# One attention and FFN kernel, two written-out orders of its work

## The chip, the cores and the metric

The kernel runs on one core of one Trainium2 chip. The core has five engines with queues of their own: TensorE (PE in the profile; its weight loads are PEld), VectorE (DVE), ScalarE (ACT), GpSimd (POOL) and SyncE (SP), which here only issues transfers. The metric is the device time of one execution in microseconds, the median over several executions.

## The reference

```
phi(x) = outer(S1 x, S2 x)            # 8 x 8 = 64 features of each 32-vector
kv  = sum_s phi(k_s) v_s              # per batch and head: 64 x 32
z   = sum_s phi(k_s)                  # 64
att = phi(q) kv / (phi(q) z + 1e-6)   # 4 batches, 4 heads, 1088 positions, 32 wide
x   = att as 4352 tokens x 128
out = (relu(x Wg) * (x Wv)) Wo        # Wg, Wv: 128 x 1536, Wo: 1536 x 128
```

Everything comes in and goes out as 32-bit floats. The FFN part runs on 16-bit operands.

## The kernel before

The work of a batch goes through stages. K: the keys are transposed on VectorE (`kt1`), multiplied with the sketches on TensorE (`ksk`), transposed back (`kt2`), multiplied to features (`kphi`, on VectorE or GpSimd), and multiplied with the values (`kv`); `kve` moves the result out of PSUM. `z`, `zc`, `w`, `wc` make the denominator's weights. Q: the same for queries (`qt1`, `qsk`, `qt2`), then `bw`, `red`, `rd`, `an` for the denominator, `qphi` for the features, a transpose (`qtr`, on TensorE or as a DMA), and `num`, whose result ScalarE writes as the FFN's input `x`. The first 512 tokens go through a shorter class of their own, `First`; its steps have an `f` ahead of their name (`f sk`, `f t2`, `f csk`, `f bw`, `f rx`, `f phi`, `f tr`, `f pt`, `f num`, `f xd`).

The FFN is cut into 102 units, numbered from 0; a unit is 512 columns of hidden work. Unit u has a gate product `g u` and a value product `v u` on TensorE, each into one PSUM bank, `relu u` on ScalarE, `h u` on VectorE (gate times value, straight from PSUM), and four output products `o u`. In 19 units ScalarE copies the value out (`vcp u`) and GpSimd multiplies (`hp u`). Units 0 to 23 hold 256 tokens and two column blocks, 24 to 95 hold 512 tokens and one. The three weights come in thirds: block 0 of each by SP in 32 bits, cast by ScalarE (`cw g0`, `cw v0`, `cw o0`, line 316); blocks 1 and 2 by GpSimd's queue (line 310). In a group of six units the first two need block 0, the next two block 1, the last two block 2.

Some lines of the profile: 367 is `st`, 370 `ws`, 375 `wq`, 491 `kt1`, 501 `ksk`, 507 `kt2`, 543 `kphi`, 654 `f sk`, 660 `f t2`, 680 `f bw`, 695 `f phi`, 780 `qsk`, 793 `qt2`, 848 `num`, 916 `g` and `v`, 921 `relu`, 925 `vcp`, 931 `h`, 936 `hp`, 944 `o`, 951 `oe`, 1015 the dummy products.

No planner runs when the kernel is built. Each step is added to a list of 857 with what it needs. A table `START` gives each step a place; all steps are issued in the order of these places, so the table fixes the order of every engine's queue at once. `BANKS` gives each of 268 uses of PSUM its bank or banks. `WARM` says before which steps TensorE gets dummy products: 128 x 128 zeros times zeros, whose result nobody reads:

```
def run(self, warm):
    order = sorted(self.ops, key=lambda o: (START[o.seq] if START else 0, o.seq))
    for o in order:
        if o.seq in WARM:
            warm(WARM[o.seq])
        o.fn()
```

An engine does its steps strictly in this order: one that must wait holds up all behind it. The step `gate` on GpSimd writes one element of a tile that the load of batch 1's keys overwrites, so SP's loads of batch 1 wait for it, and those of the later batches stand behind.

Of the kernel before, what the change touches and what calls it, by code (L numbers as in the profile page):

```python
# [29 lines left out]
Q0E = 'ACT'  # L30
RXE = ['ACT', 'DVE']
START = [
# [47 lines left out]
]  # L80
BANKS = [
# [19 lines left out]
]  # L101
WARM = {34: 29, 63: 2, 143: 14, 147: 1, 152: 9}


class Lease:
# [15 lines left out]
class Plan:  # L121
# [10 lines left out]
    def run(self, warm):  # L132
        assert not START or len(START) == len(self.ops)
# [919 lines left out]
```

## Time and profile before

| | |
|---|---|
| median of 3 executions | 101.69 us (101.67 to 102.08) |
| profiled execution, span from first to last instruction | 100.1 us |
| time around the span, median less span | 1.6 us (the page gives no other time of its own) |
| busy: PE, DVE, ACT, POOL | 94.2, 82.7, 84.1, 65.8 us |
| chain that ended last | PE 81%, ACT 6%, POOL 4%, DMA 3% |
| first FFN product | 14.58 us after the span's start |
| last product on PE begins its last run | 95.18 us; the last output copy on ACT at 96.62 us |

A busy PE is one with some product in flight. Products overlap, so a PE that is busy throughout can still do more in a stretch if its products follow closer. Times in the rows are counted from the span's start. What stands in brackets behind a row is idle time of that engine just before it, and what ended it.

### The profile page before, as it was taken

Reading aid. Unit: us, or ns where it says so; the run is one execution under the profiler, and the core shown is the slowest. Engines: PE = TensorE matmul, PEld = TensorE weight load, DVE = VectorE, ACT = ScalarE, POOL = GpSimd, SP = SyncE. Lnnn points to the kernel's source line nnn. Section 1 sums busy time; section 2 is a strip of 40 time slices with the busy share of each in tenths; the row PEclk is TensorE's granted clock in tenths of the full one; section 3 lists DMA queues with packets and bytes.
Section 4 is the critical chain, followed back from the end, with each engine's and each line's share of the span. In section 5 each row is a group of like instructions: output and inputs, shape, how many; then the busy total and the mean of one; then the engine's idle time right before and its main releaser. Section 6 shows DMA issues by size and latency. Waiting matters only on the chain.

```text
span 100.1 us, 3180 instructions
## 1 busy us (share of the span) xinstructions
PE 94.2 (94%) x1223; PEld 68.3 (68%) x1223; DVE 82.7 (83%) x175; ACT 84.1 (84%) x169; POOL 65.8 (66%) x89
## 2 busy tenths in 40 slices
PE   6999989989999999999999999999999999999950
PEld 6978969848779965557673656765676665688940
DVE  4778779999989998999998689799746879897940
ACT  3445889999799798998999999899999999998730
POOL 6029947898988999999897699935944404001700
PEclk9999999999999999999999999999999999999999
DMA  2988889999930525208664200071217305003331
GB/s 43 370 229 267 146 122 358 339 269 276 342 125 0 111 66 134 45 12 235 165 182 99 60 0 7 1 169 27 52 29 120 78 0 129 2 7 84 99 105 52
DMA packets 14799, 12.40 MB, mean 124 GB/s; under 512 B 8256, under 2 KB 12352, under 8 KB 14784
## 3 DMA queue, kind: packets, MB, share of 16 engines
q1 hardware_dynamic: 13392, 10.70, 38.5%
q0 software_dynamic: 864, 0.79, 5.8%
q10 hardware_dynamic: 528, 0.72, 2.2%
q8 instruction: 9, 0.15, 0.7%
q14 instruction: 6, 0.05, 0.2%
HBM read 9.05 MB, written 2.23 MB: 113 GB/s over the span
## 4 chain that ended last, share of the span: by engine, by line
PE 81%; ACT 6%; POOL 4%; DMA 3%; issue 1%; DVE 1%
PE ps L916 42%; PE ps L944 23%; PE ps L1015 5%; ACT g_sb L921 4%; DMA wg<-in_moe_w_gate_dram 3%; PE ps L848 3%; PE ps L501 2%; PE ps L780 2%; POOL kp L543 2%; PE ps L567 2%; ACT v_sb L925 1%; POOL fqp L695 1%; ACT qpt L840 1%; PE ps L515 1%; POOL wv L310 1%
## 5 line engine op out<-in xcount | busy, mean ns | idle before, releaser
L921 ACT ACTIVATE g_sb<-ps 128x512 f16<-128x512 f32 x102 | 56.3, 613 | 3.9 <-PE ps L916 3.2
L931 DVE TENSOR_TENSOR ht<-g_sb,ps 128x512 f16<-128x512 f16 (+1 forms) x84 | 53.5, 673 | 7.2 <-PE ps L916 5.6
L916 PE MATMUL ps<-xT,wv 128*128 128x512 f16 (+1 forms) x132 | 35.6, 332 | 0.5 <-ACT g_sb L921 0.5
L916 PE MATMUL ps<-xT,wg 128*128 128x512 f16 (+1 forms) x132 | 34.3, 332 | 0.3 <-DMA wg<-in_moe_w_gate_dram 0.3
L944 PEld LDWEIGHTS <-ht 128*128 128x128 f16 x408 | 28.0, 98 | 9.2 <-issue 0.8
L944 PE MATMUL ps<-wo,ht 128*128 128x128 f16 x408 | 33.8, 219 | 0.0
L936 POOL TENSOR_TENSOR ht<-g_sb,v_sb 128x512 f16<-128x512 f16 x19 | 21.7, 1158 | 16.4 <-ACT g_sb L921 14.9
L916 PEld LDWEIGHTS <-wg 128*128 128x128 f16 x132 | 13.6, 115 | 5.9 <-issue 2.2
L543 POOL TENSOR_TENSOR kp<-kab 128x512 f16<-128x512 f32 (+2 forms) x14 | 15.7, 1136 | 2.0 <-DVE kab L507 2.0
L916 PEld LDWEIGHTS <-wv 128*128 128x128 f16 x132 | 13.9, 114 | 3.6 <-issue 1.3
L821 POOL TENSOR_TENSOR qqp<-qan,qabc 128x1024 f16<-128x1024 f32 (+1 forms) x9 | 14.9, 1658 | 0.4
L925 ACT CAST v_sb<-ps 128x512 f16<-128x512 f32 x19 | 11.3, 601 | 0.6 <-PE ps L916 0.5
L1015 PE MATMUL ps<-zero 128*128 128x128 f16 x55 | 5.9, 285 | 1.0 <-DVE zero L292 1.0
L793 DVE STREAM_TRANSPOSE qabc<-ps 128x128 f32<-128x128 f32 (+1 forms) x12 | 5.4, 488 | 1.0 <-PE ps L780 0.6
L987 DVE STREAM_TRANSPOSE qT<-q_sb 128x544 f32<-128x544 f32 (+2 forms) x9 | 5.9, 662 | 0.4 <-DMA q_sb<-in_q_dram 0.4
L1015 PEld LDWEIGHTS <-zero 128*128 128x128 f16 x55 | 5.1, 136 | 1.3 <-DVE zero L292 1.0
L951 ACT ACTIVATE o_sb<-ps 128x512 f32<-128x512 f32 (+1 forms) x10 | 5.2, 521 | 0.7 <-PE ps L944 0.7
L801 POOL TENSOR_TENSOR bw<-qabc 128x128 f32<-128x128 f32 (+1 forms) x9 | 3.7, 412 | 2.9 <-DVE qabc L793 2.9
L815 POOL TENSOR_TENSOR qan<-qabc,qrd 128x128 f32<-128x128 f32 (+1 forms) x9 | 3.3, 372 | 3.3 <-DVE qrd L811 3.3
L861 ACT CAST xT<-ps 128x512 f16<-128x512 f32 (+1 forms) x9 | 4.7, 517 | 0.5 <-PE ps L848 0.5
L491 DVE STREAM_TRANSPOSE kT<-k_sb 128x544 f32<-128x544 f32 x6 | 4.2, 724 | 0.0
L507 DVE STREAM_TRANSPOSE kab<-ps 128x576 f32<-128x576 f32 (+2 forms) x5 | 3.3, 664 | 0.7 <-PE ps L501 0.7
(94 smaller groups left out, 77.4 us busy)
## 6 DMA issues: line engine op xcount, KB each, us to landing
k_sb<-in_k_dram SPq DMA_DIRECT2D x3, 544.0 KB, 6.1
q_sb<-in_q_dram SPq DMA_DIRECT2D x3, 544.0 KB, 4.9
out_dram<-o_sb SPq DMA_DIRECT2D x22, 64.0 KB, 1.7
v<-in_v_dram SPq DMA_DIRECT2D x6, 144.0 KB, 7.7
v<-in_v_dram SPq DMA_DIRECT2D x6, 128.0 KB, 7.6
out_dram<-o_sb SPq DMA_DIRECT2D x16, 32.0 KB, 1.8
v<-in_v_dram SPq DMA_DIRECT2D x6, 64.0 KB, 3.1
k_sb<-in_k_dram SPq DMA_DIRECT2D x1, 288.0 KB, 3.5
```

Of the source, the lines that this page charges most:

```text
L543: eng.tensor_tensor(out=self.kp[:, lo:hi].rearrange("p x g (i a c) -> p (x g i) a c", i=2, a=R), in0=a[:, :, :, None].to_broadcast([128, n ...
L793: nc.vector.transpose(self.abc[:, lo:lo + m, 2 * i2:2 * i2 + 2].rearrange("p x h f -> p h x f"), pair(ls[i2])[:, :, lo * 32:(lo + m) * 32] ...
L821: nc.gpsimd.tensor_tensor(out=self.qp[:, lo:hi].rearrange("p x g (i a c) -> p (x g i) a c", i=2, a=R), in0=self.an[:, lo * H:hi * H, :, No ...
L916: nc.tensor.matmul(bank(l)[:, y * self.W:(y + 1) * self.W], w[:, j // 4, :, j % 4], x, start=True, stop=True, skip_group_check=True)
L921: nc.scalar.activation(out=self.gs, in_=bank(l), func=ACTF.Relu)
L925: nc.scalar.copy(out=self.vs, in_=bank(l))
L931: nc.vector.tensor_tensor(out=self.ht[:, t], in0=self.gs[:, t], in1=bank(l)[:, t], op=ALU.mult)
L936: nc.gpsimd.tensor_tensor(out=self.ht, in0=self.gs, in1=self.vs, op=ALU.mult)
L944: nc.tensor.matmul(o[:, s], self.ht[:, i * 128:(i + 1) * 128], wo[:, j // 4, j % 4], start=(j == 0 and s == 0), stop=(j == NJ - 1), skip_g ...
L951: nc.scalar.mul(out=self.os[:, 0:n * DM], in_=bank(self.lo)[:, 0:n * DM], mul=1.0 / (XSCALE * XSCALE))
L987: nc.vector.transpose(qT[b][:, lo:hi], q_sb[b][:, lo:hi])
L1015: nc.tensor.matmul(PS[:, 7, 0:128], zero, zero, start=True, stop=True, skip_group_check=True)
```

## The change

The three tables are replaced. No step is added, taken away or given to another engine, and no load changes its size or its queue. What changes is each engine's order, the PSUM bank of each use, and the dummy products.

```
 START = [
-    2, 5, 0, 8, 4, 42, 10, 11, 12, 16, 18, 23, 25, 29, 3, 13, 1, 14, 33, 68, 36, 87, 20, 98, 71,
...
+    1, 5, 0, 8, 4, 40, 11, 12, 13, 14, 20, 21, 25, 27, 3, 17, 2, 34, 31, 87, 35, 93, 15, 45, 89,
...
 BANKS = [
-    (0,), (2,), (3, 4), (5, 6), (1,), (5,), (3,), (7,), (6, 7), (5,), (2,), (6,), (5, 6), (6,),
...
+    (0,), (6,), (0,1), (2,3), (3,), (2,), (2,), (3,), (0,5), (5,), (5,), (3,), (4,7), (4,), (0,),
...
-WARM = {34: 29, 63: 2, 143: 14, 147: 1, 152: 9}
+WARM = {34: 29, 61: 14}
```

Read with the names of the steps, the dummies before are 29 ahead of `st`, 14 ahead of `f sk 0`, 2 ahead of `ksk 0 4`, 1 ahead of `f csk 0` and 9 ahead of `f rT 0`. Now they are 29 ahead of `st` and 14 ahead of `ksk 0 0`, which follows `st`: 43 in place of 55. The orders of the head, up to the first FFN work, are these.

```
PE before:   29 dummies, st, 14 dummies, f sk 0, ksk 0 0, 2 dummies, ksk 0 4, f aT 1, f aT 0, z 0, sx,
             1 dummy, f csk 0, f sk 1, f csk 1, 9 dummies, f rT 0, kv 0 0, w 0, f tr 0, kv 0 2, kv 0 4,
             kv 0 6, kv 0 8, f rT 1, f tr 1, f num 0, qsk 0,4, g 2, g 0, f num 1, g 3, v 2, v 3, g 1, g 6
PE now:      29 dummies, st, 14 dummies, ksk 0 0, ksk 0 4, f sk 0, sx, f sk 1, z 0, f aT 0, f aT 1,
             kv 0 0, f csk 0, f csk 1, f tr 1, f tr 0, kv 0 2, kv 0 4, kv 0 6, kv 0 8, f rT 0, w 0,
             f num 0, f num 1, f rT 1, g 0, g 1, qsk 0,4, v 1, g 6, g 7, v 6, g 11, v 7, g 3, v 0, v 3
DVE before:  ws, qt1, kt1 0 4, kt2 0 0, f t2 0, kt2 0 4, kphi 0 2, zc 0, kphi 0 4, f bw 0, f red 0, f t2 1,
             f rd 0, f bw 1, f red 1, f rd 1, kphi 0 6, f rx 1, qt1 0 4, kve 0, f xd 0, qt2 x4, red, rd,
             f xd 1, h 2
DVE now:     ws, kt1 0 4, qt1, kt2 0 0, kt2 0 4, f t2 0, f t2 1, kphi 0 2, zc 0, kphi 0 6, kphi 0 4, f bw 0,
             f red 0, f rd 0, f bw 1, f red 1, f rd 1, f rx 1, kve 0, f xd 0, qt1 0 4, f xd 1, qt2 x4, h 1
ACT before:  table, ident, wq, vc 0 0, kbc 2, f aTe 1, f aTe 0, kbc 4, vc 0 1, L, f rx 0, cw g0, f rTe 0,
             wc 0, f pt 0, cw v0, f rTe 1, f pt 1, cw o0, relu 2, relu 0, relu 3
ACT now:     table, wq, vc 0 0, ident, kbc 2, cw o0, kbc 4, f aTe 0, f aTe 1, L, vc 0 1, f rx 0, f pt 0,
             f pt 1, f rTe 0, cw g0, cw v0, wc 0, f rTe 1, relu 1, relu 0, relu 6
POOL before: s1r, kphi 0 0, kphi 0 8, wv 1, f phi 0, wg 2, wg 1, f phi 1, wv 2, gate, bw, wo 1, wo 2, bw
POOL now:    s1r, kphi 0 0, f phi 1, f phi 0, kphi 0 8, wv 1, wg 2, wg 1, wv 2, gate, wo 1, wo 2, bw, bw
SP before:   ..., v 0, wo 0, v 0 x3, wg 0, wv 0, q 0, k 1, q 1, k 2, v 2, v 1 x2, v 2, v 1 x2, ...
SP now:      ..., wo 0, v 0 x4, wg 0, wv 0, q 0, k 1, q 1, v 1 x3, k 2, v 1, v 2, q 2, k 3, ...
```

In the POOL and SP lines a weight name or k, q, v stands for the issue of that load; the number behind is the block or the batch.

Behind the head the orders differ throughout in which unit comes when. Some places that matter for single waits: `num 0,4` of both halves and both `qtr 0,4` come after more FFN products than before; VectorE's `kt1` of batch 1 stands after `h 1`, `h 6`, `h 0` and three small steps (before: after `h 2`, `h 3`, `h 0`, `h 6`, `h 1` and two small steps); GpSimd's `kphi 1 4` and `kphi 1 0` stand ahead of batch 1's `an` and `qphi` (before: `kphi 1 4` behind them). TensorE's last steps, from `o 93` on, and the stores behind them keep their order, apart from the issue of single stores.

124 rows, old and new, of tables (BANKS, START) are left out of this document.

## The prediction

> **What bounds the kernel now.** I read the page first: the span, the busy shares, the chain that ended last.
>
> ```profile
> span 100.1 us, 3180 instructions
> PE 94.2 (94%) x1223; PEld 68.3 (68%) x1223; DVE 82.7 (83%) x175; ACT 84.1 (84%) x169; POOL 65.8 (66%) x89
> PE 81%; ACT 6%; POOL 4%; DMA 3%; issue 1%; DVE 1%
> ```
>
> TensorE ends last, and no instruction is taken from it but 12 of 55 dummies. So the question is where it waits. Three windows (columns: span, length, busy time of PE, its loads, DVE, ACT, POOL, clock, DMA share, GB/s) show that:
>
> ```profile
> 14.58:25.95 11.37, 10.59 (x125) 8.82 (x125) 11.12 (x25) 11.01 (x24) 9.60 (x13) 1.00 1.06 301
> 25.95:38.60 12.65, 12.41 (x239) 9.59 (x239) 11.77 (x25) 10.38 (x22) 11.85 (x13) 1.00 0.36 111
> 38.60:96.60 58.00, 57.95 (x639) 38.61 (x634) 49.43 (x90) 53.95 (x105) 36.09 (x36) 1.00 0.31 74
> ```
>
> From 38.60 on TensorE has 0.05 us of idle time in 58: a new order can win next to nothing there. From 14.58 to 25.95 it idles 0.78 us, while VectorE is busy 11.12 and ScalarE 11.01 of 11.37: those two set the pace. Before 14.58 no FFN product runs. So the gain must come from the head, and reach the end through VectorE and ScalarE. These rows of the timeline (start, length, engine) carry the head:
>
> ```profile
> 1.00 3.28 PE L1015 MATMUL ps<-zero 128*128 128x128 f16 x29 [1.00 <-DVE zero L292]
> 4.75 1.44 PE L1015 MATMUL ps<-zero 128*128 128x128 f16 x14
> 5.33 0.19 DVE L370 TENSOR_TENSOR wS<-ps,maskp 128x32 f32<-128x32 f32 x1 [0.70 <-ACT wq L375]
> 6.11 0.34 PE L654 MATMUL ps<-qT,wS 64*32 64x64 f32 x16
> 6.25 0.42 PE L501 MATMUL ps<-kT,wS 64*32 64x128 f32 x16
> 6.78 0.45 DVE L507 STREAM_TRANSPOSE kab<-ps 128x256 f32<-128x256 f32 x1 [0.24 <-PE ps L501]
> 7.15 0.27 DVE L660 STREAM_TRANSPOSE fab<-ps 128x128 f32<-128x128 f32 x1
> 7.31 1.66 POOL L543 TENSOR_TENSOR kp<-kab 128x512 f16<-128x512 f32 x2 [1.53 <-DVE kab L507]
> 7.43 0.52 DVE L507 STREAM_TRANSPOSE kab<-ps 128x320 f32<-128x320 f32 x1
> 7.87 0.65 DVE L543 TENSOR_TENSOR kp<-kab,ps 128x512 f16<-128x512 f32 x1
> 8.80 0.19 DVE L523 TENSOR_TENSOR zs<-ps,mz 128x32 f32<-128x32 f32 x1 [0.28 <-PE ps L515]
> 8.91 0.72 POOL L310 DMA_DIRECT2D wv<-in_moe_w_val_dram  x1
> 9.65 1.08 POOL L695 TENSOR_TENSOR fqp<-fab 128x512 f16<-128x512 f32 x1
> 9.78 0.22 DVE L680 TENSOR_TENSOR fbw<-fab,ps 128x64 f32<-128x64 f32 x1
> 10.41 0.67 PE L1015 MATMUL ps<-zero 128*128 128x128 f16 x9
> 10.61 0.40 ACT L626 COPY frx<-frd 128x256 f32<-128x256 f32 x1
> 10.67 1.13 POOL L310 DMA_DIRECT2D wg<-in_moe_w_gate_dram  x2
> 11.30 0.62 ACT L316 CAST wg<-qabc 128x512 f16<-128x512 f32 x1 [0.29 <-DMA qabc<-in_moe_w_gate_dram]
> 11.81 0.29 DVE L626 COPY frx<-frd 128x256 f32<-128x256 f32 x1
> 12.97 0.59 POOL L310 DMA_DIRECT2D wv<-in_moe_w_val_dram  x1
> 13.38 0.38 ACT L631 COPY frT<-ps 128x256 f32<-128x256 f32 x1
> 13.74 0.50 PE L780 MATMUL ps<-qT,wq 32*32 32x128 f32 x32
> 13.93 0.42 DVE L715 TENSOR_TENSOR xT<-ps,frT 128x256 f16<-128x256 f32 x1 [0.47 <-PE ps L708]
> 14.12 0.64 ACT L316 CAST wo<-qabc 128x512 f16<-128x512 f32 x1
> 14.43 0.91 DVE L793 STREAM_TRANSPOSE qabc<-ps 128x128 f32<-128x128 f32 x4
> 14.58 0.63 PE L916 MATMUL ps<-xT,wg 128*128 128x256 f16 x4 [0.34 <-DMA wg<-in_moe_w_gate_dram]
> 15.03 2.56 ACT L921 ACTIVATE g_sb<-ps 128x512 f16<-128x512 f32 x5 [0.26 <-PE ps L916]
> 16.11 0.69 DVE L931 TENSOR_TENSOR ht<-g_sb,ps 128x512 f16<-128x512 f16 x1
> ```
>
> The first gate product (14.58) waited for a weight block that POOL loads, because the old order begins with units 2 and 3, which need the second block. ScalarE's relus start at 15.03, VectorE's products at 16.11.
>
> **The change part by part.**
>
> *Dummies.* The run of 29, st and 14 stands first in both orders, so the head run is not new. The 2, 1 and 9 later ones fall. After the 9 (10.41 + 0.67 = 11.08) comes the product that needs frx, which ScalarE writes until 11.01: without them TensorE would have waited anyway. Worth: 0 to 0.67, and I take 0. Their cover is frx.
>
> *First steps.* ksk 0 0 goes ahead of f sk 0, whose start-to-start was 6.25 - 6.11 = 0.14. So VectorE's first kt2 starts at 6.78 - 0.14 = 6.64. The ws step now precedes wq instead of waiting for it; that is hidden by the 14 dummies, which hold TensorE until 6.1 in either order.
>
> *VectorE's queue to frx.* The new order is kt2, kt2, f t2, f t2, kphi, zc, kphi, kphi, f bw, f red, f rd. By start-to-start distances: 0.37 (6.78 to 7.15), 0.44 (7.43 to 7.87), twice 0.28 (7.15 to 7.43), three kphi at 0.65, zc 0.19, and 0.83 from f bw to frx (9.78 to 10.61). The sum is 4.34, so frx starts at 6.64 + 4.34 = 11.0, against 10.61. The head's beginning is thus 0.4 later.
>
> *POOL's queue.* Both f phi now precede kphi 0 8 and all weight loads. From 7.2: kphi 0 0 1.1 (1.66 less half-size kphi 0 8, some 0.58), f phi twice 1.1, kphi 0 8 0.58, giving 11.1; the wv block 0.74, two wg blocks 0.57 each, the second wv 0.59: the gate (12.97 + 0.59 = 13.56 before) falls at 13.6, and SP's loads of batch 1 behind it start as before. But the first wv is issued at 11.1, not 8.91, and the wg pair at 11.8 and 12.4, not 10.67 and 11.2. Next on POOL come both wo loads (0.57 each, to 14.7) and then bw, whose input comes later still.
>
> *ScalarE and the first product.* frx 11.0 to 11.4; two fpt, one frT, cast of wg block 0, cast of wv block 0, wc, frT. ScalarE steps 0.51 per 512 columns (2.56 / 5). So fpt at 11.4 and 11.9, frT 12.4 to 12.8, wg cast until 13.3, wv cast 13.9, wc 14.05, second frT 14.35. VectorE: second bw, red and rd (at most 0.83), frx (0.29) and kve (taken as long) to about 12.3, so num 0 follows at 12.4; xd 0 (0.42) runs from 12.8 to 13.2. The first gate product, g 0, needs xd 0 and block 0 and starts at 13.4. Block 0 itself is no wait, since its cast could begin at 11.30 before.
>
> The cast of wo block 0 (14.12, 0.64) moves to between the two kbc copies, near 7.5, and its SP load one place up. The page has no landing for it. At 5.0, as for the gate block from the same queue, and an issue at about 4.0, it lands at 9.0: ScalarE then stands until 9.7 with the second kbc behind it, which VectorE's kphi, due at 8.9, waits for: 0 to 1.1 lost on frx. I take 0, since fewer bytes stand ahead of it than of the gate block. The second x tile is ready at 14.35 + 0.42 = 14.8.
>
> *The lead.* First product 14.58 - 13.4 = 1.2 earlier. First relu at 14.35 against 15.03 (behind the frT): 0.7 earlier. VectorE: xd 1 to 14.8, the four qt2 (0.91) to 15.7, first h there against 16.11: 0.4 earlier. The lead that counts is that of the paced engines, 0.4 to 0.7; I take 0.55.
>
> *The body.* Here stand a piece of the chain (six half products in 0.66, so 0.22 for a whole one), a wait of the old order, and loads with their size and time to landing:
>
> ```profile
> 22.32 0.66 PE ps L916 x6
> 20.57 0.38 PE L916 MATMUL ps<-xT,wv 128*128 128x256 f16 x2 [0.38 <-ACT g_sb L921]
> 19.41 0.74 DVE L491 STREAM_TRANSPOSE kT<-k_sb 128x544 f32<-128x544 f32 x1
> wg<-in_moe_w_gate_dram POOLq DMA_DIRECT2D x2, 128.0 KB, 3.2
> wo<-in_moe_w_out_dram POOLq DMA_DIRECT2D x2, 128.0 KB, 7.2
> qabc<-in_moe_w_gate_dram SPq DMA_DIRECT2D x1, 256.0 KB, 5.0
> ```
>
> The new order puts num 0,4 and both qtr behind more FFN products, so a wait such as the 0.38 at 20.57 can go. Of VectorE's idle time in the first two windows, 0.25 + 0.88 = 1.13, between none and all may be recovered; I take 0.6. Against that, kt1 of batch 1 now stands behind only three h and some small steps, at about 18.3. Its load had landed by 19.41 (no wait shows there), and when is not shown: VectorE waits 0 to 1.1, and everything behind it in its queue too. I take 0.2. SP issues v of batch 1 ahead of k of batch 2 now, three issues later for the latter: 0 to 1.7 at POOL's 0.57 each, and 0 taken, since about 5 us of products lie before its use. From 38.60 on I take 0: TensorE is full in both. The tail after 96.6 keeps the same last products, from o 93 on, and their stores: 0.
>
> **Sum:** 0.55 + 0.6 - 0.2 = 0.95 us gained of the span 100.1. The page gives no time around the span; the median 101.69 lies 1.6 above it, which I keep: 101.69 - 0.95 = 100.7. With the ends (0.4 + 0 - 1.1 and 0.7 + 1.13 - 0) the parts reach from 0.7 lost to 1.8 gained: 102.4 to 99.9. TensorE's own lead of 1.2 with its idle 0.78 would be 2.0, 99.7.
>
> VectorE's frx copy (0.29, at 11.81 before, near 12.0 after) now lies beside POOL's wg issue. [...]
>
> **The rivals.**
>
> *The weight loads become the bound (slower).* g 11 is the eighth FFN product of the new order and needs the third wg block; the fourth pair needs the second. By 0.22 per product plus qsk (0.50) and the wait for the second x, TensorE comes to g 11 at about 15.5; the block, issued at 11.8, lands at 15.0 at the 3.2 of its row. Yet two blocks that POOL issued later took 7.2. At 7.2 it lands at 19.0: TensorE stops for 3.5, and ScalarE and VectorE behind it. Less the gain of 0.95 that is 2.5 lost, 104.2. It decides once the landing is later than about 16.4. For it: the loads are issued 1.1 to 2.2 later, nearer to SP's batch-1 loads. Against: those start no sooner than before, and the second wv block at 12.97 was no wait of the page's chain.
>
> *The lead is absorbed (no change).* VectorE at 98% and ScalarE at 97% in the first window, POOL at 94% in the second: a first product 1.2 earlier only makes TensorE wait for banks later. POOL starts bw at 15.8 rather than about 15.0, and kphi 1 4 and kphi 1 0 now stand ahead of the batch-1 query work; its idle time must make up for that. Time: 101.7, within 0.5.
>
> *The clock falls (slower).* The 14 dummies step 1.44 / 14 = 0.10, the later 9 only 0.67 / 9 = 0.07: the array had sped up in between, though the windows show a granted clock of 1.00. With 12 dummies fewer after 6.1 it might slow again. The climb took from the first dummy at 1.0 to the end of the 14 at most, 5.2 us (4.75 + 1.44 - 1.0); as long at 0.07/0.10 of the rate loses 1.6: 101.69 - 0.95 + 1.6 = 102.3. [...]
>
> **How the numbers follow.** Forecast, a gain of 0.5 to 2.0: 60%. Lead absorbed: 22%, of which 2 end faster and 2 slower. Weight loads: 8%. Clock: 5%. A loss of up to 0.7 by the waits bounded above (wo cast, kt1): 5%, of which 3 beyond 0.5. The predicted time is 100.7, the likeliest case's own range 99.7 to 101.2. The 8-in-10 range is 99.7 to 102.4; it holds the absorbed lead and the small losses and leaves out the late weight loads. Under 0.5% (0.5 us) either way this kernel cannot be told from no change. Faster 0.60 + 0.02 = 0.62, slower 0.08 + 0.05 + 0.03 + 0.02 = 0.18, same 0.20.
>
> **What would show it.** Right: the first gate product near 13.4 and the first relu near 14.4, the first h before 16.0, no dummies after 6.1, TensorE idle under 0.8 in the following 11 us, and the same saturation after. Wrong: a wait of TensorE for wg over 0.9 after 15; a VectorE wait over 0.5 ahead of the batch-1 key transpose (the lead is spent there); products of 128 columns stepping 0.10 after 6.1 (clock); or a head no shorter, if frx comes later than 11.4.

## The result, and the profile after

The changed kernel takes 107.97 us (107.87 to 108.77) against 101.84 us (101.67 to 102.08) for the kernel before beside it: the ratio is 1.061, with a 95% interval of 1.056 to 1.065. The forecast was 100.7 us, its range 99.7 to 102.4. Medians here are over all executions; ratios leave out the slow ones, those more than 1.5% above the fastest of their kernel. Line numbers after the change are 4 lower: 912 is `g` and `v`, 917 `relu`, 927 `h`, 940 `o`, 776 `qsk`, 789 `qt2`, 487 `kt1`, 503 `kt2`.

From the page of the changed kernel: the span, the busy shares, the chain of waits by engine, and two groups of instructions (behind the bars: busy time and mean ns, then idle time ahead and what ended most of it).

```profile
span 106.2 us, 3159 instructions
PE 94.8 (89%) x1211; PEld 68.2 (64%) x1211; DVE 83.1 (78%) x175; ACT 83.4 (78%) x169; POOL 65.6 (62%) x89
PE 63%; DMA 13%; DVE 8%; POOL 6%; ACT 3%; issue 3%; SPq 1%; DVEq 0%; ACTq 0%
L917 ACT ACTIVATE g_sb<-ps 128x512 f16<-128x512 f32 x102 | 55.5, 620 | 9.8 <-DVE qabc L789 4.2
L789 DVE STREAM_TRANSPOSE qabc<-ps 128x128 f32<-128x128 f32 (+1 forms) x12 | 6.0, 510 | 5.5 <-PE ps L912 2.8
```

The engines are as busy as before, and everything lies 6.1 us further apart. What is new is the releaser: ScalarE's relus wait for `qabc`, the result of the query transposes `qt2`, which no relu reads.

The timeline of the changed kernel, first VectorE, then TensorE, then ScalarE:

```profile
14.16 0.42 DVE L711 TENSOR_TENSOR xT<-ps,frT 128x256 f16<-128x256 f32 x1 [0.28 <-ACT frT L627]
15.14 0.32 DVE L789 STREAM_TRANSPOSE qabc<-ps 128x128 f32<-128x128 f32 x1 [0.56 <-ACT g_sb L917]
15.93 0.51 DVE L789 STREAM_TRANSPOSE qabc<-ps 128x128 f32<-128x128 f32 x2 [0.47 <-PE ps L912]
17.17 0.32 DVE L789 STREAM_TRANSPOSE qabc<-ps 128x128 f32<-128x128 f32 x1 [0.72 <-ACT g_sb L917]
17.41 2.02 DVE L927 TENSOR_TENSOR ht<-g_sb,ps 128x512 f16<-128x512 f16 x3
...
13.33 0.60 PE L912 MATMUL ps<-xT,wg 128*128 128x256 f16 x4
15.52 0.60 PE L912 MATMUL ps<-xT,wg 128*128 128x256 f16 x4 [0.63 <-DVE qabc L789]
16.50 0.41 PE L912 MATMUL ps<-xT,wv 128*128 128x256 f16 x2 [0.39 <-DVE qabc L789]
...
13.99 1.12 ACT L917 ACTIVATE g_sb<-ps 128x512 f16<-128x512 f32 x2
16.54 1.09 ACT L917 ACTIVATE g_sb<-ps 128x512 f16<-128x512 f32 x2 [1.43 <-DVE qabc L789]
```

Until 14.2 the head runs as forecast. Then the four `qt2` go by turns with FFN work that has nothing to do with them: a transpose waits for a relu, a product for the transpose, the next transpose for that product, a relu for it. They end at 17.49, not at 15.7, and the first `h` starts at 17.41.

The list of waits (us in total, times, longest) says how much of this there is in the whole span; the last line is from the list of the kernel before, its only wait of over 0.3 us of `qt2` for anything.

```profile
ACT g_sb L917 <- DVE qabc L789: 4.2, 3, 2.1
PE ps L912 <- DVE qabc L789: 3.1, 6, 0.9
DVE qabc L789 <- PE ps L912: 2.8, 5, 1.0
DVE qabc L789 <- ACT g_sb L917: 1.7, 3, 0.7
PE ps L940 <- DVE qabc L789: 1.4, 2, 0.9
...
DVE qabc L793 <- PE ps L780: 0.6, 2, 0.4
```

Three windows of the kernel before, then the same three of the changed one (length, busy PE, its loads, DVE, ACT, POOL, clock, DMA share, GB/s):

```profile
15.00:20.00 5.00, 4.84 (x44) 4.25 (x43) 4.92 (x13) 4.97 (x11) 4.09 (x8) 1.00 1.02 348
40.00:50.00 10.00, 10.00 (x94) 6.11 (x92) 9.64 (x21) 9.63 (x20) 9.64 (x12) 1.00 0.43 115
60.00:70.00 10.00, 10.00 (x104) 6.51 (x102) 9.17 (x19) 9.46 (x19) 7.35 (x9) 1.00 0.22 51
...
15.00:20.00 5.00, 3.53 (x30) 2.83 (x30) 3.39 (x10) 3.24 (x7) 1.86 (x4) 1.00 1.04 280
40.00:50.00 10.00, 8.24 (x109) 4.81 (x78) 7.66 (x17) 7.26 (x16) 7.44 (x11) 1.00 0.55 144
60.00:70.00 10.00, 9.10 (x109) 5.49 (x108) 7.93 (x17) 8.13 (x17) 9.17 (x11) 1.00 0.02 5
```

TensorE idles 1.47, 1.76 and 0.90 us in windows where it idled 0.16, 0 and 0. Query transposes stand in each of these windows, and TensorE's idle rows there wait for them: 0.63, 0.39 and 0.41 us in the first, 0.38 and 0.41 in the last, and in the second these two:

```profile
42.01 0.38 PE L940 MATMUL ps<-wo,ht 128*128 128x128 f16 x4 [0.88 <-DVE qabc L789]
43.70 0.38 PE L912 MATMUL ps<-xT,wv 128*128 128x256 f16 x2 [0.88 <-DVE qabc L789]
```

The clock is 1.00 in all of them.

The place to look is `BANKS`. A transpose `qt2` or `kt2` reads two PSUM banks in one instruction, with a step from the first to the second. In the table before, all 17 such pairs are neighbours, such as (3,4) or (6,7). In the new one 12 of the 17 are not: the first two query uses hold (2,6) and (1,5), and between their banks lie bank 3 of `g 0` and `v 6` and bank 4 of `f num 1` and `g 6`.

**Theory A:** an instruction that reads a pair is ordered against everything in the banks between the two as well. **Theory B:** the order of the queues and loads is what costs, and the banks don't matter.

### The profile page after: what moved, and what is told of

It is laid out like the page before. It is cut to its first block, busy times and chain, and to the rows that moved or that the text cites. A ratio compares the mean times of both kernels' runs of the same rounds, so it can differ in the third digit from the quotient of the medians.

```text
span 106.2 us, 3159 instructions
## 1 busy us (share of the span) xinstructions
PE 94.8 (89%) x1211; PEld 68.2 (64%) x1211; DVE 83.1 (78%) x175; ACT 83.4 (78%) x169; POOL 65.6 (62%) x89
## 4 chain that ended last, share of the span: by engine, by line
PE 63%; DMA 13%; DVE 8%; POOL 6%; ACT 3%; issue 3%; SPq 1%; DVEq 0%; ACTq 0%
PE ps L912 37%; PE ps L940 19%; DMA k_sb<-in_k_dram 10%; DVE qabc L789 4%; DMA qpt<-qqp 3%; POOL fqp L691 2%; DVE kab L503 2%; PE ps L844 2%; ACT g_sb L917 2%; POOL kp L539 2%; PE ps L776 1%; POOL wv L306 1%; DVE ht L927 1%; POOL wg L306 1%; PE ps L563 1%
## 5 line engine op out<-in xcount | busy, mean ns | idle before, releaser
L917 ACT ACTIVATE g_sb<-ps 128x512 f16<-128x512 f32 x102 | 55.5, 620 | 9.8 <-DVE qabc L789 4.2
L912 PE MATMUL ps<-xT,wv 128*128 128x256 f16 (+1 forms) x132 | 34.4, 331 | 1.8 <-DVE qabc L789 1.7
L539 POOL TENSOR_TENSOR kp<-kab 128x512 f16<-128x512 f32 (+2 forms) x14 | 15.7, 1132 | 1.0 <-DVE kab L503 1.0
L817 POOL TENSOR_TENSOR qqp<-qan,qabc 128x1024 f16<-128x1024 f32 (+1 forms) x9 | 14.8, 1658 | 0.5
L789 DVE STREAM_TRANSPOSE qabc<-ps 128x128 f32<-128x128 f32 (+1 forms) x12 | 6.0, 510 | 5.5 <-PE ps L912 2.8
L1011 PE MATMUL ps<-zero 128*128 128x128 f16 x43 | 4.5, 295 | 1.0 <-DVE zero L288 1.0
L1011 PEld LDWEIGHTS <-zero 128*128 128x128 f16 x43 | 4.1, 139 | 1.0 <-DVE zero L288 1.0
L563 PEld LDWEIGHTS <-kp 128*128 128x128 f16 x72 | 3.4, 98 | 1.0 <-issue 0.2
```

Source lines behind the costliest of these rows:

```text
L539: eng.tensor_tensor(out=self.kp[:, lo:hi].rearrange("p x g (i a c) -> p (x g i) a c", i=2, a=R), in0=a[:, :, :, None].to_broadcast([128, n ...
L789: nc.vector.transpose(self.abc[:, lo:lo + m, 2 * i2:2 * i2 + 2].rearrange("p x h f -> p h x f"), pair(ls[i2])[:, :, lo * 32:(lo + m) * 32] ...
L817: nc.gpsimd.tensor_tensor(out=self.qp[:, lo:hi].rearrange("p x g (i a c) -> p (x g i) a c", i=2, a=R), in0=self.an[:, lo * H:hi * H, :, No ...
L912: nc.tensor.matmul(bank(l)[:, y * self.W:(y + 1) * self.W], w[:, j // 4, :, j % 4], x, start=True, stop=True, skip_group_check=True)
L917: nc.scalar.activation(out=self.gs, in_=bank(l), func=ACTF.Relu)
L1011: nc.tensor.matmul(PS[:, 7, 0:128], zero, zero, start=True, stop=True, skip_group_check=True)
```

## The experiments

Each is a change of the kernel before or of the changed one; the ratios are to the kernel before.

**Banks renamed, nothing else.** In the kernel before each bank b becomes 3b mod 8, so no two uses share a bank that did not before, and every pair ends up 3 or 5 apart.

```
 BANKS = [
-    (0,), (2,), (3, 4), (5, 6), (1,), (5,), (3,), (7,), (6, 7), ...
+    (0,), (6,), (1, 4), (2, 7), (3,), (7,), (1,), (5,), (2, 5), ...
```

> The kernel before, with its order, dummies and loads untouched; only the eight PSUM banks are renamed (bank b becomes 3b modulo 8, in every use, the dummies' too). Every pair of banks that one VectorE transpose reads was two neighbours before and lies three or five banks apart now. Theory A (a step that reads two banks apart is held in order against work in the banks between them): slower by 3 to 8 us, 105 to 110 us, with VectorE's two-bank transposes waiting for relus and products of banks in between. Theory B (the order of the engines or of the loads cost the 6 us): 101.8 us, no change.

Measured: 110.31 us (110.15 to 110.33), ratio 1.082 (1.078 to 1.086). Its list of waits has the same new kind of rows (its line numbers are one above the kernel before's: 794 is `qt2`, 508 `kt2`, 922 `relu`, 917 `g` and `v`, 945 `o`):

```profile
ACT g_sb L922 <- DVE qabc L794: 2.8, 3, 1.9
PE ps L917 <- DVE qabc L794: 2.4, 4, 0.7
PE ps L945 <- DVE kab L508: 1.6, 2, 0.9
```

The names of the banks alone cost 8%, without any change of order. Theory A stands; B cannot explain this.

**Banks mirrored.** The control: b becomes 7 - b, and neighbours stay neighbours.

> The kernel before with every PSUM bank b renamed to 7-b, so that all 17 two-bank pairs stay neighbours. Theory A (a transpose that reads two banks holds everything in the banks between them): nothing lies between neighbours, so the time stays at the time before, 101.5 to 102.5 us. Rival (some banks, or any renaming, are bad by themselves, which would explain the 110.3 us of the other renaming as well): several us slower, 104 us or more.

Measured: 102.18 us (101.92 to 104.18), ratio 1.004 (1.000 to 1.008). The longest of its transposes' waits is the one the kernel before has too:

```profile
DVE qabc L794 <- PE ps L781: 0.6, 2, 0.4
```

So it is not renaming, nor certain banks, but the distance in a pair.

**One-bank reads.** In the changed kernel every transpose of a pair that is not a neighbour becomes two, of one bank each; 14 instructions more on VectorE.

```
+            if ls[i2].banks[1] - ls[i2].banks[0] > 1:
+                for h in range(2):
+                    nc.vector.transpose(
+                        self.abc[:, lo:lo + m, 2 * i2 + h],
+                        bank(ls[i2], h)[:, lo * 32:(lo + m) * 32].rearrange(...))
+                return
             nc.vector.transpose(
                 self.abc[:, lo:lo + m, 2 * i2:2 * i2 + 2].rearrange("p x h f -> p h x f"),
                 pair(ls[i2])[:, :, lo * 32:(lo + m) * 32].rearrange(...))
```

> The kernel after, with its order, banks, dummies and loads untouched; each transpose that reads two banks that aren't neighbours is issued as two transposes of one bank each (14 more VectorE instructions). Theory A: the false waits go, 102 to 104 us, since the 14 instructions cost VectorE up to 1 us. Theory B: 108 to 109 us.

Measured: 103.12 us (102.14 to 106.05), ratio 1.009 (1.005 to 1.012). Of the changed kernel's loss of 6.1% some 5.2 points are gone. From the page, the waits, and the timelines of VectorE and TensorE (797 is `qt2`, 939 `h`, 487 `kt1`, 924 `g` and `v`, 497 `ksk`):

```profile
span 100.3 us, 3176 instructions
...
DVE qabc L797 <- PE ps L782: 0.3, 1, 0.3
...
14.65 1.17 DVE L797 STREAM_TRANSPOSE qabc<-ps 128x64 f32<-128x64 f32 x8
15.74 1.25 DVE L939 TENSOR_TENSOR ht<-g_sb,ps 128x512 f16<-128x512 f16 x2
20.13 1.37 DVE L487 STREAM_TRANSPOSE kT<-k_sb 128x544 f32<-128x544 f32 x2 [1.05 <-DMA k_sb<-in_k_dram]
...
17.34 0.41 PE L924 MATMUL ps<-xT,wg 128*128 128x256 f16 x2 [1.35 <-DMA wg<-in_moe_w_gate_dram]
21.64 0.72 PE L497 MATMUL ps<-kT,wS 64*32 64x288 f32 x16 [1.48 <-DVE qrd L819]
```

No relu and no FFN product waits for a query transpose any more, and the first `h` starts at 15.74. What shows now is what lay beneath: a wait for the weights of `g 3` until 17.34, and one for the keys of batch 1 until 20.13, with TensorE's `ksk` behind it. The wait of the transposes is written into the program. As built, the first of the four transposes waits on a semaphore of TensorE and one of ScalarE in the changed kernel, and on TensorE alone here:

```
changed:   L789 STREAM_TRANSPOSE qabc<-ps 128x2x2x32 [waits PE, Activation]
one bank:  L797 STREAM_TRANSPOSE qabc<-ps 128x2x32   [waits PE]
```

The ScalarE step that it waits for is `relu 0`, which reads bank 3; the pair holds banks 1 and 5. The second transpose of this pair waits for the product `g 6` into bank 4.

**Neighbouring pairs.** In the changed kernel 44 of the 268 bank uses are given other banks, so that all pairs are neighbours; the rest stays.

> The kernel after, with its order, dummies and loads untouched; 44 of the 268 bank uses get other banks, so that all two-bank uses are neighbours. Theory A: 100 to 102 us, the time that the order was forecast to give, plus what tighter reuse of banks costs. Theory B: about 108 us.

Measured: 104.4 us, ratio 1.027 (1.020 to 1.035). The 100 to 102 us expected of theory A were missed. It mends the greater part too, though less than the one-bank reads. In its profile no relu and no FFN product waits for a query transpose, and the waits for `wg` (1.68 us) and for the keys of batch 1 (0.84) are there again. The uses that made room now follow others in their new banks; whether that is the difference of 1.3 us wasn't tried.

**The load order alone.** In the kernel before, the two moves of loads that the change makes: `wo1` and `wo2` directly behind the gate, and three loads of v of batch 1 ahead of k of batch 2.

> The kernel before, with the order of its loads alone taken from the kernel after: SP issues three value loads of batch 1 ahead of the keys of batch 2, and GpSimd both wo blocks straight behind the gate, ahead of bw. Theory A: 101.5 to 102.3 us, no change. Theory B, in its form that the loads come late (key load of batch 2 landing 10 us after its issue): slower by 2 us or more.

Measured: 105.89 us, ratio 1.030 (1.022 to 1.038). Against theory A alone, which has no place for this: the load order is a second cost, at least in the old order. The next two take it apart.

```
 SP:    ld k1, ld q1,
-       ld k2, ld v20, ld v12, ld v10, ld v23, ld v11, ...
+       ld v10, ld v12, ld v11, ld k2, ld v20, ld v23, ...
```

> The kernel before with three loads of v of batch 1 issued ahead of k of batch 2; wo1 and wo2 stay where they are. Theory K (the whole loss of the changed load order comes from k2, which landed at 26.4 us there and held the second transpose of k by 2.2 us and TensorE by 2.2): 104.5 to 106.0 us, as with both load moves (105.9). Theory W (the two early wo loads are what delays k2, since they share the 16 DMA engines with it): 101.7 to 102.5 us.

Measured, with this alone: 105.48 us (102.67 to 106.82). Three of the four executions took 105.03 to 106.82 at a mean granted clock of 0.982 to 0.984, the fourth 102.67 at 0.995; so no ratio is given.

```
 POOL:  gate,
-       bw 0,4 0 2, ld wo1, ld wo2,
+       ld wo1, ld wo2, bw 0,4 0 2,
```

> The kernel before with wo1 and wo2 issued directly behind the gate, at about 13.0 us instead of 15.3; the order on SyncE is as before. Theory K: no change, 101.7 to 102.5 us. Theory W: 104 to 106 us, with k2 landing after 25 us.

Measured, with that alone: 102.1 us (101.89 to 105.8), ratio 1.001 (0.998 to 1.003). So of the two moves it is that of k2 that can cost, though not in every execution. First its issue and its use in the kernel before, then, with the v loads ahead, its issue, VectorE's wait for it and that of TensorE's `qsk` (787) behind it:

```profile
14.58 0.38 SPq L394 DMA_DIRECT2D k_sb<-in_k_dram  x1
24.14 0.73 DVE L491 STREAM_TRANSPOSE kT<-k_sb 128x544 f32<-128x544 f32 x1
...
15.99 0.38 SPq L401 DMA_DIRECT2D k_sb<-in_k_dram  x1
26.67 0.75 DVE L498 STREAM_TRANSPOSE kT<-k_sb 128x544 f32<-128x544 f32 x1 [2.69 <-DMA k_sb<-in_k_dram]
28.74 1.17 PE L787 MATMUL ps<-qT,wq 32*32 32x256 f32 x32 [2.73 <-DVE wq L539]
```

The issue moves by 1.4 us, yet the data lands 10.7 us after it (26.67 - 15.99). In the kernel before it lands 7.0 us after its issue, at 21.6, and is used at 24.14 without a wait. So a delay of 1.4 us at the issue grows to 5.1 at the landing. Why isn't shown by a row: the three v loads that now stand ahead are 128 or 144 KB each, but with `wo` early alone k2 also takes 9.9 us, landing at 24.2, just ahead of its use at 24.31.

**The loads put back, in the changed order.** On the version with one-bank reads: k2 directly behind q1, then `wo1` and `wo2` behind `bw`, then both.

> The changed kernel with one-bank transposes, and the load of k of batch 2 moved from behind three v loads to directly behind q of batch 1, as it stands before. Theory L1 (the late k2 costs time, as it did in the kernel before with the changed load order): 101.5 to 102.5 us, below the 103.1 us of the one-bank version. Theory L2 (in this order of products the weights of the second and third tile, issued together with the two output-weight loads, are what comes late): no change, 103.1 us within 0.5.

> The changed kernel with one-bank transposes, and the loads wo1 and wo2 moved back behind the two bw operations on GpSimd. Theory L2 (the two early wo loads take bandwidth from wg, which lands at 17.3 us in the one-bank version while the product that needs it could start at 16.0; and from k1, which lands at 20.1): the 1.35 us wait for wg falls under 0.3 us and the time to 101.0 to 102.3 us. Theory L1: no change, 103.1 us within 0.5. A loss is possible where wo1 itself, landing some 7 us after about 16.5, comes after its first use at about 23 us.

> The changed kernel with one-bank transposes and both load moves undone. If the two load effects add up: 100.5 to 101.8 us, which would be below the kernel before (102.0). If neither matters, 103.1 us.

Measured: 102.23 us (ratio 0.996, 0.991 to 1.000), 102.3 us (0.998, 0.994 to 1.002) and 102.52 us (0.996, 0.991 to 1.001). Either move brings the repaired order back to the time of the kernel before; together they bring no more. The sum expected of the two (100.5 to 101.8) was a miss by the median. Their fastest executions (100.93, 101.27 and 100.97 us) lie below the fastest of 35 of the kernel before beside them (101.48), so part of the forecast lead may be there in some executions; that wasn't tried further. With `wo` late the profile shows a wait for `wg` of 0.3 us at most instead of 1.35, as expected; but in two later versions with the same load order it is 1.52 and 1.54 again, so one profile each doesn't settle what makes that landing late. The wait for k1 stays, and in the profile with both moves it is 2.67 us (below).

**The loads put back, banks as they are.** The same two moves on the changed kernel itself.

> The changed kernel with its two-bank reads as they are, and only the load order undone (k2 directly behind q1; wo1 and wo2 behind the bw operations). If the two costs are separate and add up: 106.7 to 107.3 us, 0.6 to 1.2 below the changed kernel (108.0), as the load moves gave on the one-bank version. If the stalls on the banks hide the late loads: 107.7 to 108.5 us.

Measured: 107.93 us (107.41 to 109.0), ratio 1.058 (1.052 to 1.065). Nothing is gained: while the banks stall the engines, the loads have time to land. In the changed kernel TensorE waits 0.16 us for `wg` and VectorE 0.33 for k1, against 1.35 and 1.05 with one-bank reads. The two costs don't add up; the second only shows once the first is gone.

**The 12 dummies.** The kernel before without its later dummies of 2, 1 and 9.

```
-WARM = {34: 29, 63: 2, 143: 14, 147: 1, 152: 9}
+WARM = {34: 29, 143: 14}
```

> The kernel before with the 12 later dummy products (2, 1 and 9) taken out, the first 43 kept. The prediction's step: worth nothing, since TensorE then waits in their place for the same frx copy: 101.6 to 102.3 us. Rival (the 12 keep TensorE busy enough that the clock isn't lowered in the first 12 us): the granted clock falls to about 0.5 for some us near 8 us, as the profile of one variant of the changed kernel shows, and the time is 103 us or more.

Measured: 103.56 us (102.81 to 105.16), ratio 1.013 (1.007 to 1.018). TensorE's timeline, then three windows:

```profile
10.86 1.22 PE L687 MATMUL ps<-id,frx 128*128 128x128 f32 x4 [0.77 <-ACT frx L626]
...
10.00:11.00 1.00, 0.23 (x2) 0.15 (x1) 0.89 (x5) 0.80 (x3) 1.00 (x3) 0.84 1.03 219
11.00:12.00 1.00, 1.00 (x7) 0.94 (x8) 1.00 (x2) 0.59 (x1) 0.99 (x2) 0.50 0.63 56
...
17.00:18.00 1.00, 1.00 (x8) 0.55 (x7) 0.93 (x6) 1.00 (x2) 0.87 (x3) 0.75 0.97 290
```

TensorE waits for frx in the dummies' place, as the prediction said. But the clock then falls to 0.50 near 10.7 and stays there until about 17.5, and the first FFN product starts at 16.28 against 14.58. The fall is not all of the loss, though: the one execution at a mean clock of 1.000 still took 102.81 us, where the kernel before beside it took 101.97 (101.68 to 102.68). How the 1.3% divides isn't shown.

**More dummies and later keys.** On the version with one-bank reads and both loads put back: 22 dummies in the second run instead of 14. Then besides these the key transposes of batch 1 and their products some steps later. A first form of the latter, with the transposes behind the load of k3, which reuses k1's buffer, transposed the wrong keys and waited 9.9 us for k3, so its 113.61 us say nothing on the question.

> The changed kernel with one-bank transposes and both load moves undone (102.5 us), and 8 more dummies in its second run (22 instead of 14), which fill most of the 0.76 us in which TensorE stands idle at 5.3 us. Theory C (too few dummies at the head let the clock fall in some executions, as taking 12 away from the kernel before did): 101.0 to 101.8 us, granted clock 1.00 until 20 us. Rival (the head's clock is not at stake in this order): 102.5 us within 0.5.

> The changed kernel with one-bank transposes, both load moves undone, and besides: the two transposes of k of batch 1 put behind h 2 on VectorE, its sketch products behind o 1 on TensorE, and 8 more dummies in the second run (51 in all). Where the wait of 1.3 to 2.7 us for k1 at 19.7 to 22.4 us is what keeps the variants at 102.2 to 102.5 us: that wait falls under 0.8 us and the time to 99.5 to 101.0 us, below the kernel before. Where the work behind it was covering something else, 102 us as without these moves.

> The same with 22 dummies, and besides the two transposes of k of batch 1 behind h 2 on VectorE, the sketch products of batch 1 behind o 1 on TensorE, and the load of k of batch 3, which reuses the buffer, behind these transposes. Where the wait of 1.2 to 2.7 us for k1 (until 19.1 to 20.9 us) is what is left: TensorE's wait there falls under 0.8 us and the time to 99.5 to 101.0 us. Where what lies behind is limited by something else: the same time as with 22 dummies alone.

Measured: 102.89 us with more dummies (ratio 0.999, 0.996 to 1.003); 102.86 us with the keys later as well (1.003, 1.000 to 1.007). Neither helps: the dummies' cover isn't what the changed order lacks, and with the keys later TensorE waits 0.77 and 0.74 us at 20.8 and 22.4 instead of 2.25 us once. What keeps these versions from the forecast time stays open. No version here is surely faster than the kernel before.

## Why the prediction was wrong, point by point

- **The bound, and "from 38.60 on I take 0".** Reading a full TensorE as safe was wrong. It was full because its partners came in time. The bank waits return at the later groups of query transposes: 1.76 us idle between 40 and 50, 0.90 between 60 and 70.
- **First steps, VectorE's queue, POOL's queue, first product.** Right: frx at 11.08 (said 11.0), the first weight issue at 10.92 (11.1), the gate at 13.20 (13.6), the first product at 13.33 (13.4). The first relu, at 13.99, comes 0.36 sooner than said. VectorE's frx copy (11.68) ran beside POOL's two `wg` issues (11.64), which took 1.07 us against 1.13 before, so nothing was stretched.
- **"VectorE: xd 1 to 14.8, the four qt2 (0.91) to 15.7, first h there".** This is the step that failed. The second x ended at 14.58, in time; the four took until 17.49. They were priced at their durations, and new banks for 242 of the 268 uses were not priced at all: the sum had no term for `BANKS`. That term is 8.3 us in the old order by the renaming (110.31 less 102.0), and about 4.9 in the new one by the one-bank reads (107.97 less 103.12). The lead of 0.55 turned into a lag: the first h starts at 17.41, against 16.11 before. With one-bank reads it starts at 15.74, as the sum had it, so the durations were right and the bank waits were what was missing.
- **"k2 ... 0 to 1.7, and 0 taken".** In the old order three of four executions with this move took 3.1 to 4.9 us more than the 101.97 beside it, the fourth 0.7. The upper bound counted only three issues, and the landing moved by 5.1 us. In the changed kernel it cost nothing that shows, since putting the loads back gained nothing.
- **"kt1 waits 0 to 1.1, 0.2 taken".** Right in kind: 0.33 us at 20.14 in the changed kernel. Without the bank stalls it is 1.05 to 2.6 in four of the profiles, beyond the bound. So this term, and the wait for `wg` taken as none, are what the profile of the one-bank version (103.12 us) shows against the forecast. With the loads put back the time is still 102.2 to 102.5, and that rest is open.
- **Dummies "worth 0".** The cover was right, the worth was not: in the old order the time without them is 1.3% longer, and the clock fell in three of the four executions (mean 0.965 to 0.976). In the new order the clock was 1.00 in the profile, and more dummies, tried on the repaired version, changed nothing.
- **wo cast and tail, 0.** Nothing shows against these.
- **The rivals.** None was the one that came. *Weight loads late*, with a point of 16.4 for `g 11`, has its mechanism in the one-bank version, but with the other `wg` block. `g 11` (the seventh FFN product there, not the eighth) starts at 15.40 without a wait, where 15.5 was said. `g 3` needs the block issued second, at 11.83, which landed 5.5 us later: it starts at 17.34 after 1.35 us. In the changed kernel only 0.16 of it shows. *The clock falls* happened in the old order without its dummies, and once in the new head: in the profile of the one-bank version with k2 first, where the clock is 0.74 from 7 to 8 us and 0.50 from 8 to 17. *Lead absorbed* was nearest in form, with the wrong absorber and no price below zero.

## What to carry to other kernels

Where a table of PSUM banks changes, read first which instructions take two banks at once and what lives in the banks between: a wait there cost both sides, ScalarE 4.2 us and TensorE 3.1 for the transposes and these 1.7 and 2.8 for them, and no row of the old profile showed it. A price of zero for a load that moves down its queue needs its time to landing, not only its issue: here that grew from 7.0 to 10.7 us. And after a large stall is mended, expect a second one beneath it, whose price the first had hidden: here waits of 1.35 and 1.05 us for loads, against 0.16 and 0.33.

## What the runs showed of the hardware

The traces tell something of the clock. Here are TensorE's wait for k1 in the version with one-bank reads and both loads put back, and three windows behind it:

```profile
22.37 0.72 PE L506 MATMUL ps<-kT,wS 64*32 64x288 f32 x16 [2.67 <-DVE qrd L828]
...
23.00:24.00 1.00, 1.00 (x17) 0.95 (x10) 1.00 (x3) 0.41 (x1) 1.00 (x2) 0.62 1.16 321
24.00:25.00 1.00, 1.00 (x11) 0.87 (x9) 0.84 (x2) 0.38 (x2) 1.00 (x2) 0.50 1.10 257
...
26.00:27.00 1.00, 1.00 (x23) 0.39 (x20) 0.84 (x2) 0.89 (x3) 1.00 (x2) 0.67 1.02 277
```

If the clock is only ever 1.00 or 0.50, as the rows within a fall suggest, a window of 1 us whose mean clock is c spent 2(1 - c) us at half speed; what follows is an estimate from the rows on that footing. Here that is 0.76 + 2 + 0.66 = 3.42 us (the row of 25 to 26 has 0.50 too). With the v loads ahead of k2 the rows of 28 to 33 us have 0.82, three times 0.50, and 0.97: 0.36 + 3 + 0.06 = 3.42. Without the 12 dummies it is 0.32 + 6 + 0.50 = 6.82, twice that. In the profiled execution of the version with k2 first, which took 104.37 us, it is 0.52 + 9 + 0.72 = 10.24, three times. Why the four falls stand as one to one to two to three, no run here shows.

What sets off a fall isn't shown either. By the same estimate one began 0.2 us before the end of a wait of 0.77 us (the 12 dummies; 0.50 us more of idle time lie between 5 and 10), one 0.3 us after the second of two waits of 0.48 and 0.81 us (k2 first), one 0.9 us after a wait of 2.67 us (both loads put back), and one 0.1 us before the end of a wait of 2.73 us (the v loads ahead of k2). The changed kernel's 1.47 us of idle time between 15 and 20 brought none, nor did its two waits of 0.88 us between 40 and 50: the clock is 1.00 there. So no one length of wait parts the falls from the rest in these traces.
